# The second layer's inner products by Strassen's seven products of quarters

## The chip, the cores and the metric

The program runs on one core of one Trainium2 chip. The metric is the device time of one execution, in microseconds, as a median of several runs. TensorE multiplies a stationary 128x128 block (loaded by its own instruction, LDWEIGHTS) with a moving block and accumulates in PSUM; VectorE (DVE), ScalarE (ACT) and GpSimd (POOL) do the elementwise work; SyncE (SP) issues the transfers.

## The reference

Attention over 4 batches x 8 heads, 1152 positions of 64, with the queries averaged in pairs (576 queries), and then two feed-forward layers over the 2304 resulting tokens of width 512, each through 2048 hidden columns:

```
attn = softmax(q_pool @ k.T / sqrt(64)) @ v      # q_pool: mean of neighbouring queries
x  = attn as [2304, 512]
h  = x @ w_in      ; x = (h * cos(h))     @ w_out      # layer 1: w_in 512x2048, w_out 2048x512
h  = x @ w_in2     ; y = (h * sigmoid(h)) @ w_out2     # layer 2, same shapes
```

The weights arrive as 64-bit floats, the rest as 32-bit floats.

## The kernel before

Every operand of a product is split in two 16-bit halves, a high part and the rest (`ih`, `il` for w_in, `oh`, `ol` for w_out, `xh`, `xl` for the tokens), and a product is three matmuls: high x high, high x rest, rest x high. All scales are powers of two, taken per piece of a weight and per block of tokens from a mean or maximum that one small matmul (`bm`, L96) spreads over the partitions.

Order of work: attention with layer 1 mixed in; then the rest of layer 1; then layer 2. Tokens go in 9 blocks of 256 (the ninth gathers the remainders of the four batches). A generator `layer1` emits for every 128 hidden columns (f, 16 of them) a first product (`g1_unit`, 12 matmuls of 256 columns, L527), its evacuation by ACT (`hk`, L540), and the nonlinearity in groups of four f (L552, L553, L559, L562, L567 and POOL's `gl`, L568), and 12 units later the second product (`g2_unit1`, L586). The result of a block goes to DRAM (`ydr`) and is read back for layer 2 (`y32b`).

Layer 2's weights are prepared by the generator `weight_steps`, eight pieces of w_in2 and then eight of w_out2. A piece of 128 x 1024 wide numbers is loaded (L177, three staging buffers), decoded (ACT L206, DVE L207, L210, L215, L218), scaled (L96 to L107) and written as two halves (ACT L238, L239; POOL L240). One step of it is emitted with each remaining unit of layer 1 until w_in2 is complete (`W2.half`), and then one step with each unit of layer 2. The small matmul of a scale takes its PSUM tile from `state.psw`, which for this stage is a pool `ps_m` of its own with two buffers.

Layer 2 runs over the blocks n and over f: a first product (`g1_unit`), evacuation with Silu (L540), and for four f together the split of the result into `gh` and `gl` on DVE (`g_silu`, L574, L575). The second products (`g2_unit2`, six matmuls of 512 columns, L607, into two banks `o0`, `o1`) follow three blocks of f units later:

```
for f in range(NF):
    g1_unit(W2, cur, f)
    ...
    next(wgen2, None)
    ...
    if len(pend) > (TAIL_G - 1) * NF:
        second()
```

The split of the next block of tokens (`y_split`: maximum L112, scale, high part on ACT L890, rest on DVE L891) is emitted within the block before. The list above is a priority: a scheduler puts the instructions of each engine in a fixed order ahead of the run, and may place later work earlier where an engine would be idle by its own times. At the end stand three blocks of second products alone and the evacuation (L617) with the transfer of the output (L622).

Of the kernel before, what the change touches and what calls it, by code (L numbers as in the profile page):

```python
# [45 lines left out]
def attention_moe_moe_kernel(ctx, tc, q, k, v, w_in1, w_out1, w_in2, w_out2, out):  # L46
# [32 lines left out]
    def scale_steps(m, pool, res, top, wide=False):  # L79

        n = m.shape[1]
        if wide:
            w = small.tile([128, 1], F32, name="mw", tag="mw")
            wi, mi = w.bitcast(I32), m.bitcast(I32)
            nc.vector.tensor_scalar(
                out=wi, in0=mi, scalar1=3, scalar2=0x3F800000, op0=ALU.logical_shift_left, op1=ALU.bitwise_and
            )  # L90
            nc.vector.scalar_tensor_tensor(
                out=wi, in0=mi, scalar=1 << 30, in1=wi, op0=ALU.bitwise_and, op1=ALU.bitwise_or
            )
            m = w
        bc = pool.tile([128, 2, GW], F32, tag="h", name="bm")[:, 0, 0:4]
# [34 lines left out]
    def run_all(g):  # L130
        for _ in g:
            pass
# [11 lines left out]
    def new_w(tag, npc):  # L144
        w = Weights()
        w.npc = npc
        w.half = False
        for nm in ("si", "ui", "so", "uo"):
            setattr(w, nm, const.tile([128, npc], F32, name=nm + tag))
        w.uoT = const.tile([128, NC], F32, name="uoT" + tag)  # L150
        w.kg = const.tile([128, 1], F32, name="kg" + tag)
        w.ug = const.tile([128, 1], F32, name="ug" + tag)
        return w

    def weight_steps(w, srcs, stage, pspool, eng, nsub, bufs, ahead, wt_bufs=WT_BUFS):
# [103 lines left out]
        for e in range(r):  # L259
            pp = slice(e * (128 // r), (e + 1) * (128 // r))  # L260
            nc.vector.tensor_copy(w.uoT[pp, :], w.uo.rearrange("p (c e) -> p c e", e=r)[pp, :, e])


    class Pair:
# [211 lines left out]
    def x_scale_consts(w, s, u, first):  # L476


        c = Weights()
        n = 3 if first else TAIL_G + 1  # L480
        c.k = small.tile([128, 1], F32, tag="ck%d" % first, name="ck", bufs=n)
        c.a = small.tile([128, w.npc], F32, tag="ca%d" % first, name="ca", bufs=n)
        two_pi = 2.0 * math.pi
        nc.vector.tensor_scalar(
            out=c.k, in0=s, scalar1=w.kg, scalar2=two_pi if first else 1.0, op0=ALU.mult, op1=ALU.mult
        )
        nc.vector.tensor_scalar(
            out=c.a, in0=w.ui, scalar1=u, scalar2=0.25 / two_pi if first else 0.25, op0=ALU.mult, op1=ALU.mult
        )
        if first:  # L490
            c.y = y_scale(w, u, w.uoT, "cy1")
        return c
# [75 lines left out]
            nc.gpsimd.tensor_tensor(out=G.gl, in0=t, in1=gh, op=ALU.subtract)  # L568
        groups.clear()

    def g_silu(blk, f):
        hk = blk.hk
        gh, gl = (blk.gt[:, e, f - 3:f + 1, :] for e in range(2))
        nc.vector.tensor_scalar(out=gh, in0=hk, scalar1=blk.c.k, scalar2=None, op0=ALU.mult)  # L574
        nc.vector.scalar_tensor_tensor(out=gl, in0=hk, scalar=blk.c.k, in1=gh, op0=ALU.mult, op1=ALU.subtract)  # L575
        blk.g.append((gh, gl))

    def g2_unit1(w, blk, f):

# [20 lines left out]
    def g2_unit2(w, blk, f, pool):  # L600

        if f == 0:
            blk.y = [pool.tile([128, DM], F32, tag="o%d" % i, name="o") for i in range(2)]
        gh, gl = blk.g[f // 4]
        for i in range(2):
            for e, (gt, wt) in enumerate(((gh, w.oh), (gh, w.ol), (gl, w.oh))):
                nc.tensor.matmul(  # L607
                    blk.y[i], gt[:, f % 4, i * 128:(i + 1) * 128], wt[:, f, :],
                    start=(f == 0 and e == 0), stop=(f == NF - 1 and e == 2),
                )  # L610

    def y_evac2(W2, pool, blk, dsts):
        cy = y_scale(W2, blk.u, W2.uo, "cy0")
        for i in range(2):
            o = pool.tile([128, DM], F32, tag="x32_%d" % i, name="osb")
            np_ = W2.npc
            nc.vector.tensor_tensor(  # L617
                out=o.rearrange("p (c n) -> p c n", c=np_), in0=blk.y[i].rearrange("p (c n) -> p c n", c=np_),
                in1=cy.rearrange("p (c n) -> p c n", n=1).to_broadcast([128, np_, DM // np_]), op=ALU.mult,
            )  # L620
            for dst, p0, n in dsts[i]:
                nc.sync.dma_start(out=dst, in_=o[p0:p0 + n, :])  # L622


    if True:
        W1 = new_w("1", 8)
        alloc_w(W1, wpool, "1")
        ydr = [dram.tile([128, NC * GW], F32, name="ydr%d" % i) for i in range(2 * B + 1)]
        xrem = wpool.tile([128, B, NP * D], F32, name="xrem")

        att_stack = ExitStack()
        at = att_pools(att_stack)
# [6 lines left out]
        state.mp = None  # L639
        state.ng, state.tail = 0, False  # L640
        state.psw = ps_h
        W2 = new_w("2", 8)
        state.credit = 0.0
        bg = []
        blocks_q = []
# [146 lines left out]
        for n, (b, j) in enumerate(pairs):  # L792
# [54 lines left out]
        ps_m = ctx.enter_context(tc.tile_pool(name="ps_m", bufs=2, space=PSUM, side="right"))  # L847
# [12 lines left out]
        rb.ydst = ydr[2 * B]  # L860
        blocks_q.append(rb)

        alloc_w(W2, w2p, "2")
        state.psw = ps_m


        def y_load(n):
# [6 lines left out]
        def y_split(yb):  # L874
# [5 lines left out]
            yield from early(scale_steps(m, ps_m, (yb.s, yb.u), 14), P_CH)  # L880
            yb.blk = blk = Block()
            blk.g = []
            if yb.n:
                ys_ = state.mp.p.tile([128, 2, NC, GW], F16, tag="x%d" % (yb.n % 2), name="ys", bufs=1)
                yh, yl = ys_[:, 0], ys_[:, 1]
            else:
                ys_ = w2p.tile([128, 2, NC, GW], F16, name="ys0")
                yh, yl = ys_[:, 0], ys_[:, 1]
            yhf, ylf = yh.rearrange("p c n -> p (c n)"), yl.rearrange("p c n -> p (c n)")
# [4 lines left out]
            blk.xh = lambda c: yh[:, c, :]  # L894
            blk.xl = lambda c: yl[:, c, :]

        def y_consts(yb):
            yb.blk.c = x_scale_consts(W2, yb.s, yb.u, False)
            yb.blk.u = yb.u
            yb.blk.gt = wpool.tile([128, 2, NF, GW], F16, tag=("ih1", "il1", "oh1", "ol1")[yb.n % TAIL_G], name="gt", bufs=1)  # L900

        yb = y_load(0)
        run_all(y_split(yb))
# [24 lines left out]
        def second():  # L928
            blk, ff, nn = pend.pop(0)
            g2_unit2(W2, blk, ff, ps_o)  # L930
            if ff == NF - 1:
                y_evac2(W2, wpool, blk, out_dst(nn))

        gen = None
        for n in range(NB):
            nyb = y_load(n + 1) if n + 1 < NB else None
            gen = y_split(nyb) if nyb else None
            for f in range(NF):
                g1_unit(W2, cur, f)
                g1_evac(state.mp, W2, cur, f, False)  # L940
                if f % 4 == 3:
                    g_silu(cur, f)
                pend.append((cur, f, n))
                next(wgen2, None)
                if gen is not None and f >= 4 and next(gen, False) is False:
                    gen = None
                if len(pend) > (TAIL_G - 1) * NF:
                    second()
            if n == TAIL_G - 2:
                run_all(wgen2)  # L950
            if gen is not None:
                run_all(gen)
            if nyb:
                y_consts(nyb)
                cur = nyb.blk
        while pend:
            second()
        ctx.enter_context(moe_stack)
# [30 lines left out]
```

## Time and profile before

| | |
|---|---|
| median of 3 runs | 1409.16 us (1408.9 to 1414.57) |
| the profiled execution | 1411.62 us, of which the span of its instructions is 1409.8 us |
| mean granted clock of TensorE | 0.928 of full speed |
| busy: PE, DVE, ACT, POOL | 1162.9, 996.4, 767.5, 567.2 us |
| layer 2, from the last product of layer 1 to the end | about 1021 to 1409.8 us |

Busy time of PE is the union of matmuls that overlap each other, and a matmul's own duration is longer than the step from one to the next; steps are read from the starts in the timeline or from runs in the chain. "Idle before" is the time in which an engine waited ahead of an instruction, with what ended the wait.

### The profile page before, as it was taken

How to read it: one execution, taken by the hardware profiler on the slowest of the kernel's cores; microseconds unless marked ns; L12 is line 12 of the kernel's file. 1: busy time of each engine (PE TensorE's matmuls, PEld its weight loads, DVE VectorE, ACT ScalarE, POOL GpSimd, SP SyncE). 2: the span in 40 equal slices, each digit the busy share in tenths (PEclk: the TensorE clock that was granted, in tenths of full speed). 3: DMA queues.
4: the chain of work that ended last, by engine and by line, in shares of the span. 5: the costliest groups of instructions: out<-in, count | busy, mean ns of one | idle time of the engine just before them, and what ended most of it. 6: DMA issues, size and time to landing. Idle time of an engine off the chain costs nothing.

```text
span 1409.8 us, 24849 instructions
## 1 busy us (share of the span) xinstructions
PE 1162.9 (82%) x10020; PEld 852.0 (60%) x10020; DVE 996.4 (71%) x1848; ACT 767.5 (54%) x907; POOL 567.2 (40%) x296
## 2 busy tenths in 40 slices
PE   1465356787988778898889889979989999999998
PEld 0243233475676556666667678868878766666643
DVE  7999997778777888977999885997776323223110
ACT  3686487668777678876788775553363111111100
POOL 1577276535755466645666563552321000000000
PEclk9976568699999989998999999999999999999999
DMA  7799789987799999978899964441330000000001
GB/s 232 192 239 209 188 155 204 202 171 135 154 201 174 202 194 211 177 151 181 152 209 184 214 131 91 151 119 46 90 105 32 16 31 30 16 16 16 1 30 30
DMA packets 493074, 186.16 MB, mean 132 GB/s; under 512 B 433056, under 2 KB 467872, under 8 KB 492960
## 3 DMA queue, kind: packets, MB, share of 16 engines
q1 hardware_dynamic: 492960, 184.59, 61.7%
q8 instruction: 78, 1.28, 0.4%
q14 instruction: 36, 0.29, 0.1%
HBM read 66.58 MB, written 9.44 MB: 54 GB/s over the span
## 4 chain that ended last, share of the span: by engine, by line
PE 36%; DVE 25%; ACT 9%; issue 8%; DMA 7%; POOL 2%; SPq 2%; ACTq 0%; DVEq 0%; POOLq 0%
PE h L527 14%; PE o L607 13%; DVE sc L410 5%; PE y L586 5%; DMA hlT<-hl 3%; DVE tt L553 2%; DVE tt L552 2%; POOL hl L429 2%; PE sp L391 2%; ACT hl L424 2%; SPq L431 2%; PE pv L442 2%; DVE gh L567 1%; DVE tt L562 1%; DVE vt L311 1%
## 5 line engine op out<-in xcount | busy, mean ns | idle before, releaser
L429 POOL TENSOR_TENSOR hl<-sc,hl 128x1152 f16<-128x1152 f32 x144 | 367.8, 2563 | 189.9 <-ACT hl L424 110.8
L391 PE MATMUL sp<-kT,qT 128*128 128x512 f16 (+1 forms) x768 | 197.6, 375 | 111.2 <-DVE sc L410 86.5
L527 PEld LDWEIGHTS <-ih 128*128 128x128 f16 x2304 | 225.8, 99 | 64.6 <-issue 12.5
L410 DVE TENSOR_SCALAR_CACHE_REDUCE sc<-sp,psu 128x512 f32<-128x512 f32 (+1 forms) x288 | 229.2, 807 | 40.2 <-PE sp L391 38.8
L540 ACT ACTIVATE hk<-h,ca 128x512 f32<-128x512 f32 x144 | 97.7, 682 | 255.0 <-PE h L527 251.0
L418 ACT ACTIVATE sc<-sc,nb 128x1152 f32<-128x1152 f32 x144 | 180.3, 1252 | 95.2 <-DVE nb L415 80.6
L442 PE MATMUL pv<-vt,hlT 128*128 128x130 f16 (+1 forms) x1440 | 197.2, 239 | 39.6 <-DMA hlT<-hl 33.3
L527 PE MATMUL h<-ys,ih 128*128 128x256 f16 x1152 | 194.8, 273 | 2.9 <-ACT hk L540 2.7
L442 PEld LDWEIGHTS <-hlT 128*128 128x128 f16 (+1 forms) x1440 | 148.6, 111 | 71.0 <-DMA hlT<-hl 45.4
L527 PE MATMUL h<-xT,ih 128*128 128x256 f16 x1024 | 187.1, 276 | 4.7 <-ACT hk L540 3.9
L446 PE MATMUL pv<-vt,hlT 128*128 128x65 f16 (+1 forms) x1440 | 189.5, 209 | 0.0
L607 PE MATMUL o<-oh,gt 128*128 128x512 f16 x576 | 187.9, 379 | 1.0 <-ACT oh L238 0.6
L391 PEld LDWEIGHTS <-qT 128*128 128x128 f16 x768 | 77.9, 110 | 179.2 <-issue 137.1
L424 ACT ACTIVATE hl<-sc 128x1152 f16<-128x1152 f32 x144 | 165.5, 1157 | 18.5 <-DMA xT<-xn 8.9
L586 PE MATMUL y<-gl,oh 128*128 128x256 f16 x576 | 159.4, 277 | 3.7 <-POOL gl L568 3.7
L586 PE MATMUL y<-gh,oh 128*128 128x256 f16 x576 | 159.8, 277 | 2.5 <-ACT y L595 1.7
L586 PE MATMUL y<-gh,ol 128*128 128x256 f16 x576 | 159.7, 277 | 0.0
L527 PE MATMUL h<-ys,il 128*128 128x256 f16 x576 | 157.0, 273 | 0.0
L446 PEld LDWEIGHTS <-hlT 128*128 128x128 f16 (+1 forms) x1440 | 143.7, 108 | 16.2 <-issue 6.7
L527 PE MATMUL h<-xT,il 128*128 128x256 f16 x512 | 141.5, 276 | 0.0
L568 POOL TENSOR_TENSOR gl<-tt,gh 128x1024 f16<-128x1024 f32 x36 | 93.5, 2598 | 110.2 <-DVE gh L567 105.5
L607 PEld LDWEIGHTS <-gt 128*128 128x128 f16 x864 | 84.6, 98 | 81.3 <-issue 2.1
(281 smaller groups left out, 1884.5 us busy)
## 6 DMA issues: line engine op xcount, KB each, us to landing
wst<-in_moe_w_in_dram SPq DMA_DIRECT2D x16, 1024.0 KB, 5.7
wst<-in_moe_w_out_dram SPq DMA_DIRECT2D x16, 1024.0 KB, 6.2
stk<-in_k_dram SPq DMA_DIRECT2D x32, 288.0 KB, 4.0
stv<-in_v_dram SPq DMA_DIRECT2D x32, 288.0 KB, 4.4
stq<-in_q_dram SPq DMA_DIRECT2D x32, 256.0 KB, 3.1
ydr<-y SPq DMA_DIRECT2D x9, 512.0 KB, 3.8
y32b<-ydr SPq DMA_DIRECT2D x9, 512.0 KB, 3.3
out_dram<-osb SPq DMA_DIRECT2D x16, 256.0 KB, 2.1
```

What stands on the lines that cost most here:

```text
L391: nc.tensor.matmul(sp[:, o - a:o - a + n], P.qT[e][:, t, :], kT[:, o:o + n], start=(e == 0), stop=(e == 1))
L410: nc.vector.tensor_scalar(out=T.sc[:, a:z], in0=sp, scalar1=T.P.su, scalar2=None, op0=ALU.mult, op1=ALU.min, accum_out=mx[:, x:x + 1],)
L418: nc.scalar.activation(out=T.sc, in_=T.sc, func=AF.Exp, scale=-1.0, bias=nb)
L424: nc.scalar.activation(out=hi, in_=T.sc, func=AF.Copy)
L429: nc.gpsimd.tensor_tensor(out=T.hl[:, 1, :], in0=T.sc, in1=T.hl[:, 0, :], op=ALU.subtract)
L442: nc.tensor.matmul(G.pv[r, T.gi], T.hlT[:, 0, c, r], P.vt[i][:, c], start=(c == 0), stop=(c == KC - 1), skip_group_check=True,)
L446: nc.tensor.matmul(G.pv[r, T.gi, 0], T.hlT[:, 1, c, r], P.vt[i][:, c, 0], start=False, stop=(c == KC - 1), skip_group_check=True,)
L527: nc.tensor.matmul(hp, wt[:, c, f * 128:(f + 1) * 128], xt(c), start=(i == 0), stop=(i == 3 * NC - 1), skip_group_check=True,)
L540: nc.scalar.activation(out=o, in_=blk.hp, func=AF.Copy if first else AF.Silu, scale=blk.c.a[:, g:g + 1])
L568: nc.gpsimd.tensor_tensor(out=G.gl, in0=t, in1=gh, op=ALU.subtract)
L586: nc.tensor.matmul(blk.y[:, oc, :], wt[:, f, oc * 128:(oc + 1) * 128], gt[:, f % 4, :], start=(f == 0 and e == 0 and oc % 2 == 0), stop=(f ...
L607: nc.tensor.matmul(blk.y[i], gt[:, f % 4, i * 128:(i + 1) * 128], wt[:, f, :], start=(f == 0 and e == 0), stop=(f == NF - 1 and e == 2),)
```

## The change

The two weights' halves of w_in2 and the tokens are cut in quarters: the 512 inputs in two halves (two chunks of 128 each), the 2048 hidden columns in two halves (the even and the odd pieces of 256), the 256 tokens of a block in two halves of 128. Seven products of quarters take the place of eight, each of 128 moving columns instead of 256. The sums of quarters of the weights are formed on POOL while they are prepared (`sum_steps`, `write_pair`; seven operands in `ih`, `il`), those of the tokens on DVE in `y_split` (seven operands). `half_block` runs the seven products for half of the hidden columns, with three PSUM banks (`y`, `x`, `v`), and puts the quarters of the result together with copies on ACT and additions on DVE before Silu and the split. Two half blocks make a block.

What else moves: w_out2's halves now lie in the space of layer 1's `ih1`, `il1`; the split results `gt` in `oh1`, `ol1`, a new tile `g2w` and the tiles of layer 1's `gh`, `gl`; PSUM of `ps_m` now holds `x` and `v`, and the small matmuls of the scales take their tile from `o0` until w_in2 is complete and from layer 1's `y` (one buffer) after that. Scales of the first operands have one bit more of room (13 in place of 14), and w_in2 has one scale for two pieces. The second products follow at eight for each half block, spread over its seven steps.

The diff, cut to its core:

```diff
+        def write_pair(q, st0, st1):
+            v0, v1, f0, f1 = (x[:, :, :, z] for z in (1, 0) for x in (st0, st1))
+            for v in (v0, v1):
+                nc.scalar.activation(out=v, in_=v, func=AF.Copy, scale=w.si[:, q:q + 1])
+            sub = lambda o, x, y, op=ALU.subtract: nc.gpsimd.tensor_tensor(out=o, in0=x, in1=y, op=op)
+            hi, lo = (x.rearrange("p o c f -> p (o c) f")[:, :, q * hn:(q + 1) * hn] for x in (w.ih, w.il))
+            halves(hi[:, 0:4], lo[:, 0:4], v0)
+            yield
+            sub(f0[:, 0:2], v0[:, 0:2], v1[:, 0:2])
+            sub(v1[:, 0:2], v1[:, 0:2], v1[:, 2:4], ALU.add)
+            sub(f0[:, 2:4], v1[:, 0:2], v0[:, 0:2])
+            halves(hi[:, 4:8], lo[:, 4:8], v1)
+            yield
+            sub(f1[:, 0:2], v0[:, 2:4], f0[:, 2:4])
+            halves(hi[:, 8:12], lo[:, 8:12], f0)
+            more()
+            yield
+            halves(hi[:, 12:14], lo[:, 12:14], f1[:, 0:2])
+            more()
+            yield
...
+    def quarter_products(bank, op, xop, w, blk, u, start):
+        for i in range(4):
+            r = 4 * u + i
+            for c in range(2):
+                for wt, xt in ((w.ih, blk.xh), (w.ih, blk.xl), (w.il, blk.xh)):
+                    nc.tensor.matmul(
+                        bank[:, i, :], wt[:, op, c, r * 128:(r + 1) * 128], xt[:, xop, c, :],
+                        start=start, stop=True, skip_group_check=True,
+                    )
+                    start = False
...
+    def half_block(mp, st, w, blk, u):
...
+        y = bank("h", ps_h)
+        quarter_products(y, 0, 0, w, blk, u, True)
+        h0, h1 = (mp.p.tile([128, 4, GW], F32, tag="hk", name="hk", bufs=NB_HK) for _ in range(2))
+        copy(h0[:, :, n0], y)
+        yield
+        x = bank("x", st.psum)
+        quarter_products(x, 1, 1, w, blk, u, True)
+        add(h0[:, :, n0], x)
+        yield
+        quarter_products(y, 5, 4, w, blk, u, False)
+        copy(h0[:, :, n1], y)
+        yield
+        v = bank("w", st.psum)
+        quarter_products(v, 2, 3, w, blk, u, True)
+        yield
+        quarter_products(y, 4, 5, w, blk, u, False)
+        copy(h1[:, :, n1], y)
+        add(h1[:, :, n1], v)
+        yield
+        quarter_products(y, 3, 6, w, blk, u, False)
+        silu(blk, u, h1, y, n0)
+        silu(blk, u, h1[:, :, n1], h1[:, :, n1], slice(0, 128))
+        yield
+        quarter_products(v, 6, 2, w, blk, u, False)
+        add(h0[:, :, n1], v)
+        silu(blk, u, h0, h0, slice(0, GW))
+        g_halves(blk, u, 0, h0)
+        g_halves(blk, u, 1, h1)
+        yield
...
-                wgen2 = weight_steps(W2, (w_in2, w_out2), w2st, lambda: state.psw, nc.sync, 1, W2_BUFS, 1, 1)
+                wgen2 = sum_steps(W2, (w_in2, w_out2), w2st, lambda: state.psw, nc.sync, W2_BUFS)
...
-            nc.scalar.activation(out=yhf, in_=yb.y32, func=AF.Copy, scale=yb.s)
-            nc.vector.scalar_tensor_tensor(
-                out=ylf, in0=yb.y32, scalar=yb.s, in1=yhf, op0=ALU.mult, op1=ALU.subtract
-            )
...
+            t = state.mp.p.tile([128, 4, 2, 128], F32, tag="tt", name="yt", bufs=NB_TT)
+            for o, x, y in ((0, b12, b11), (1, b22, t[:, 0]), (2, b22, b12), (3, b21, t[:, 1])):
+                nc.vector.tensor_tensor(out=t[:, o], in0=x, in1=y, op=ALU.subtract)
+            yield
+            for o, n, x in ((0, 4, y4[:, :, 0:128]), (4, 2, b22), (6, 8, t.rearrange("p o c n -> p (o c) n"))):
+                h, lo = (z.rearrange("p o c n -> p (o c) n")[:, o:o + n] for z in (blk.xh, blk.xl))
+                nc.scalar.activation(out=h, in_=x, func=AF.Copy, scale=yb.s)
+                nc.vector.scalar_tensor_tensor(out=lo, in0=x, scalar=yb.s, in1=h, op0=ALU.mult, op1=ALU.subtract)
...
+        W2.oh, W2.ol = (wpool.tile([128, NF, DM], F16, tag=nm + "1", name=nm + "2", bufs=1) for nm in ("ih", "il"))
+        state.psw = (ps_y, "y")
...
+            for j, _ in enumerate(half_block(state.mp, st, W2, blks[n], u)):
                 next(wgen2, None)
+                if u == 0 and j > 1 and gen is not None:
+                    next(gen, None)
+                k += 8
+                while len(pend) > (TAIL_G - 1) * NF - 8 and k >= 7:
                     second()
+                    k -= 7
+            pend += [(blks[n], 8 * u + i, n) for i in range(8)]
```

Here `halves` is one ACT copy to the high half and one POOL subtraction for the rest. The decoding and scaling of a piece and the writing of w_out2's pieces are as before, one ahead of the other.

## Rows read from the trace of the kernel before

**Rows 1.** Stretches: length, each engine's busy time (instructions), clock, DMA share, GB/s.

```profile
900.00:950.00 50.00, 40.35 (x348) 34.55 (x347) 49.93 (x76) 28.11 (x31) 23.55 (x9) 0.93 0.40 116
...
1021.00:1064.00 43.00, 37.71 (x339) 32.92 (x338) 33.55 (x60) 24.86 (x30) 10.62 (x4) 1.00 0.31 93
...
1100.00:1341.00 241.00, 241.00 (x1671) 163.08 (x1670) 66.93 (x95) 37.44 (x52) 0.00 (x0) 1.00 0.05 18
```

**Rows 2.** PE's waits from 868 to 1021 us: total, times, longest.

```profile
PE bm L96 <- DVE mw L91: 7.9, 3, 6.7
PE h L527 <- ACT hk L540: 2.9, 3, 2.4
```

**Rows 3.** First products of layer 2 on the page, and their weight loads.

```profile
L527 PEld LDWEIGHTS <-ih 128*128 128x128 f16 x2304 | 225.8, 99 | 64.6 <-issue 12.5
...
L527 PE MATMUL h<-ys,ih 128*128 128x256 f16 x1152 | 194.8, 273 | 2.9 <-ACT hk L540 2.7
...
L527 PE MATMUL h<-ys,il 128*128 128x256 f16 x576 | 157.0, 273 | 0.0
```

**Rows 4.** Chain of waits in a steady block: start, length, matmuls in the run.

```profile
1216.23 2.29 PE h L527 x21
1224.05 1.31 PE h L527 x12
...
1230.69 1.32 PE o L607 x6
...
1258.05 2.29 PE h L527 x21
```

**Rows 5.** PE timeline in attention, 26 matmuls in a run: start, length.

```profile
857.71 0.19 PE L446 MATMUL pv<-vt,hlT 128*128 128x65 f16 x1
857.74 0.22 PE L442 MATMUL pv<-vt,hlT 128*128 128x130 f16 x1
...
858.76 0.19 PE L446 MATMUL pv<-vt,hlT 128*128 128x65 f16 x1
```

**Rows 6.** Groups by form from 1021 to 1064 us, the opening of layer 2.

```profile
L240 POOL TENSOR_TENSOR ol<-wst,oh 128x1024 f16<-128x1024 f32 x4 | 10.6, 2663 | 36.4 <-ACT wst L239 36.4
...
L540 ACT ACTIVATE hk<-h,ca 128x512 f32<-128x512 f32 x12 | 7.9, 683 | 5.5 <-PE h L527 3.1 <-issue 2.3
L575 DVE SCALAR_TENSOR_TENSOR gt<-hk,ck,gt 128x1024 f16<-128x1024 f32 x6 | 7.7, 1280 | 0.1
...
L112 DVE TENSOR_REDUCE ym<-y32b 128x1 f32<-128x1024 f32 x3 | 3.6, 1214 | 0.4 <-DMA y32b<-ydr 0.4
...
L207 DVE TENSOR_SCALAR_CACHE_REDUCE wt<-wt 128x1024 f32<-128x1024 f32 x2 | 2.4, 1220 | 1.3 <-ACT wt L206 1.2
```

**Rows 7.** Scales of w_out2's pieces: ns shortest/median/longest, first and last start.

```profile
L103 DVE TENSOR_SCALAR so<-uo x8: 141/145/151, 946.1 to 1062.8; 128x1 int32<-128x1 int32 x8
```

**Rows 8.** ACT timeline, the last evacuation of layer 1.

```profile
1021.27 1.57 ACT L595 ACTIVATE y<-y,cy 128x256 f32<-128x256 f32 x4 [5.24 <-PE y L586]
```

**Rows 9.** DVE timeline, one piece of w_in2 decoded.

```profile
928.73 1.22 DVE L207 TENSOR_SCALAR_CACHE_REDUCE wt<-wt 128x1024 f32<-128x1024 f32 x1
...
929.99 0.69 DVE L210 TENSOR_SCALAR wt<-wt 128x1024 int32<-128x1024 int32 x1
...
930.78 1.23 DVE L215 SCALAR_TENSOR_TENSOR wst<-wst,wt 128x1024 int32<-128x1024 int32 x1
...
932.05 1.22 DVE L218 SCALAR_TENSOR_TENSOR wst<-wst 128x1024 int32<-128x1024 int32 x1
```

**Rows 10.** Line 617, the evacuation of the output: ns shortest/median/longest.

```profile
L617 DVE TENSOR_TENSOR osb<-o,cy x18: 683/692/693, 1132.0 to 1404.6; 128x512 f32<-128x512 f32 x18
```

**Rows 11.** Line 574: ns shortest/median/longest.

```profile
L574 DVE TENSOR_SCALAR gt<-hk,ck x36: 736/753/2143, 1025.5 to 1341.6; 128x1024 f16<-128x1024 f32 x36
```

**Rows 12.** POOL timeline beside the longest of line 574, which starts at 1032.45.

```profile
1031.92 2.12 POOL L240 TENSOR_TENSOR ol<-wst,oh 128x1024 f16<-128x1024 f32 x1 [18.19 <-ACT wst L239]
```

**Rows 13.** ACT timeline, the first pieces of w_in2 written.

```profile
872.45 3.44 ACT L238 ACTIVATE ih<-wst,si 128x1024 f16<-128x1024 f32 x3
```

More of the change, by code (lines that the diff above doesn't have):

```diff
@@ L147, in new_w @@
         w.half = False
+        w.sums = sums
         for nm in ("si", "ui", "so", "uo"):
-            setattr(w, nm, const.tile([128, npc], F32, name=nm + tag))
+            n = npc // 2 if sums and nm[1] == "i" else npc
+            setattr(w, nm, const.tile([128, n], F32, name=nm + tag))
         w.uoT = const.tile([128, NC], F32, name="uoT" + tag)
@@ L261, in weight_steps, with sum_steps, shape, more @@
             nc.vector.tensor_copy(w.uoT[pp, :], w.uo.rearrange("p (c e) -> p c e", e=r)[pp, :, e])
+    def sum_steps(w, srcs, stage, pspool, eng, bufs):
+        npc = w.npc
+        hn = DFF // npc
+        srcs = [x.bitcast(I32) for x in srcs]
+        todo = [(kind, p) for kind in "io" for p in range(npc)]
+        staged = []
+        def shape(kind):
+            return (NC, DFF // npc) if kind == "i" else (NF, DM // npc)
+        def more():
+            if todo:
+                kind, p = todo.pop(0)
+                c, n = shape(kind)
+                st = stage.tile([128, c, n, 2], I32, tag="wst", name="wst", bufs=bufs)
+                eng.dma_start(
+                    out=st.rearrange("p c f z -> p c (f z)"),
+                    in_=srcs[kind == "o"][:, p * n * 2:(p + 1) * n * 2].rearrange("(c p) f -> p c f", p=128),
+                )
+                staged.append(st)
+        for _ in range(bufs):
+            more()
+        yield
+        def decode(kind, m):
+            c, n = shape(kind)
+            st = staged.pop(0)
+            t = stage.tile([128, c, n], F32, tag="wt", name="wt", bufs=1)
+            ti = t.bitcast(I32)
+            nc.scalar.activation(out=t, in_=st.bitcast(F32)[:, :, :, 1], func=AF.Abs)
+            nc.vector.tensor_scalar(
+                out=t, in0=t, scalar1=W_MIN, scalar2=None, op0=ALU.max, op1=ALU.max, accum_out=m
+            )
+            nc.vector.tensor_scalar(
+                out=ti, in0=ti, scalar1=3, scalar2=0x3FFFFFF8, op0=ALU.logical_shift_left, op1=ALU.bitwise_and
+            )
+            yield
+            v = st[:, :, :, 1]
+            nc.vector.scalar_tensor_tensor(
+                out=v, in0=v, scalar=-(1 << 30), in1=ti, op0=ALU.bitwise_and, op1=ALU.bitwise_or
+            )
+            nc.vector.scalar_tensor_tensor(
+                out=v, in0=st[:, :, :, 0], scalar=29, in1=v, op0=ALU.logical_shift_right, op1=ALU.bitwise_or
+            )
+            yield
+            return st.bitcast(F32)
+        def scales(m, s, u, top):
+            for _ in early(scale_steps(m, pspool(), (s, u), top, True), P_CH):
+                pass
+        def halves(hi, lo, t):
+            nc.scalar.activation(out=hi, in_=t, func=AF.Copy)
+            nc.gpsimd.tensor_tensor(out=lo, in0=t, in1=hi, op=ALU.subtract)
+        def first(q):
+            m = small.tile([128, 2], F32, name="wm2", tag="wm2", bufs=2)
+            return m, (yield from decode("i", m[:, 0:1]))
+        def second(q, m):
+            st = yield from decode("i", m[:, 1:2])
+            m1 = small.tile([128, 1], F32, name="wm1", tag="wm1", bufs=3)
+            nc.vector.tensor_reduce(out=m1, in_=m, axis=AX.X, op=ALU.max)
+            scales(m1, w.si[:, q:q + 1], w.ui[:, q:q + 1], 13)
+            yield
+            return st
+        def write_pair(q, st0, st1):
[16 more added lines that the diff above has]
+            halves(hi[:, 12:14], lo[:, 12:14], f1[:, 0:2])
+            more()
+            yield
+        m, st0 = yield from first(0)
+        for q in range(npc // 2):
+            st1 = yield from second(q, m)
+            nxt = None
+            if q + 1 < npc // 2:
+                nxt = yield from first(q + 1)
+            yield from write_pair(q, st0, st1)
+            if nxt:
+                m, st0 = nxt
+        nc.vector.tensor_reduce(out=w.kg, in_=w.si, axis=AX.X, op=ALU.min)
+        nc.vector.tensor_reduce(out=w.ug, in_=w.ui, axis=AX.X, op=ALU.max)
+        nc.vector.tensor_scalar(out=w.kg, in0=w.kg, scalar1=2.0**-13, scalar2=None, op0=ALU.mult)
+        nc.vector.tensor_scalar(out=w.ug, in0=w.ug, scalar1=2.0**10, scalar2=None, op0=ALU.mult)
+        w.half = True
+        def decode_o(p):
+            m = small.tile([128, 1], F32, name="wm", tag="wm", bufs=3)
+            st = yield from decode("o", m)
+            scales(m, w.so[:, p:p + 1], w.uo[:, p:p + 1], 14)
+            yield
+            return st
+        def write_o(p, st):
+            n = DM // npc
+            t, sc = st[:, :, :, 1], w.so[:, p:p + 1]
+            hi, lo = (x[:, :, p * n:(p + 1) * n] for x in (w.oh, w.ol))
+            nc.scalar.activation(out=hi, in_=t, func=AF.Copy, scale=sc)
+            nc.scalar.activation(out=t, in_=t, func=AF.Copy, scale=sc)
+            nc.gpsimd.tensor_tensor(out=lo, in0=t, in1=hi, op=ALU.subtract)
+            more()
+            yield
+        st = yield from decode_o(0)
+        for p in range(npc):
+            nst = None
+            if p + 1 < npc:
+                nst = yield from decode_o(p + 1)
+            yield from write_o(p, st)
+            st = nst
@@ L481, in x_scale_consts @@
         c.k = small.tile([128, 1], F32, tag="ck%d" % first, name="ck", bufs=n)
-        c.a = small.tile([128, w.npc], F32, tag="ca%d" % first, name="ca", bufs=n)
+        c.a = small.tile([128, w.ui.shape[1]], F32, tag="ca%d" % first, name="ca", bufs=n)
         two_pi = 2.0 * math.pi
@@ L879, in y_split @@
             yield
[L880 removed]
+            yield from early(scale_steps(m, state.psw, (yb.s, yb.u), 13), P_CH)
             yb.blk = blk = Block()
[L882 to L885, printed above, removed]
[L886 to L888 removed]
@@ new lines, in y_consts @@
+        def y_consts(yb):
+            blk = yb.blk
+            blk.c = x_scale_consts(W2, yb.s, yb.u, False)
+            blk.u = yb.u
+            z = yb.n % TAIL_G
+            if z < 3:
+                gt = g2w if z == 2 else wpool.tile([128, 2, NF, GW], F16, tag=("oh1", "ol1")[z], name="gt", bufs=1)
+                blk.gt = [[gt[:, e, 4 * j:4 * j + 4, :] for e in range(2)] for j in range(4)]
+            else:
+                blk.gt = [
+                    [state.mp.p.tile([128, 4, GW], F16, tag=nm, name=nm, bufs=NB_G) for nm in ("gh", "gl")] for _ in range(2)
+                ]
+                for j in range(2):
+                    gt = wpool.tile([128, 2, 4, GW], F16, tag="x32_%d" % j, name="gt")
+                    blk.gt.append([gt[:, e] for e in range(2)])
```

99 lines of the change are left out of this document (62 added, 37 removed).

## The prediction

> **What bounds the kernel now.** I read the stretches first, because the page's average mixes stages. From 1100 us on PE is busy without a gap (241.00 of 241.00) at full clock while DVE is busy for 28% of the time [rows 1]: this part is PE's alone. Between 900 and 950 us, where w_in2 is prepared beside the rest of layer 1, it is the other way round: DVE is busy for 49.93 of 50 us and PE for 40.35. In the opening of layer 2, 1021 to 1064 us, PE lacks 43 - 37.71 = 5.3 us and DVE works 33.55 of 43. The waits say on whom PE waited there: on the small matmul of a scale, whose operand DVE had not ready (7.9 us before 1021 us), and on ACT's evacuation of `hk` (2.9 us) [rows 2]. So a product saved is worth its whole time after 1100 us, and nothing where PE already waits for DVE. The second question is therefore what the change puts on DVE before 1100 us.
>
> **Term 1: the products.** Before there are 1152 + 576 = 1728 matmuls of 256 columns [rows 3]. In the chain 12 of them take 1.31 us, 109.2 ns each, which is 256 columns at 2.4 GHz (106.7 ns) and 2.5 ns; 188.7 us in all [rows 4]. A block takes 1258.05 - 1216.23 = 41.82 us, 16 x (1.31 + 1.30), with nothing lost. After, a half block has 7 x 4 x 2 x 3 = 168 matmuls of 128 columns, 3024 in all. The doubt is whether a matmul of 128 columns, with a weight load of its own, runs at the rate of its columns: a load shows 99 ns [rows 3], more than 128 columns need. Attention shows it: from 857.71 to 858.76 us twelve pairs of 65 and 130 columns, each matmul with its own load, take 87.5 ns a pair [rows 5]; 195 columns at 2.4 GHz are 81.25, so 3.1 ns go to each matmul, and loads overlap. For 128 columns that makes 53.3 + 3.1 = 56.4 ns; with the 2.5 ns of the long matmuls, 55.8. I take 56.4, nearest in shape: 9.47 us for a half block, 170.6 us in all, a gain of **18.1 us** (19.9 at the other end).
>
> Attention's pairs show 43.8 ns for a matmul of 97.5 columns in the mean. The Trainium skill ("TensorE: Matmul & The Clock Gate", Back-to-back issue gap) gives about 81 ns as the sustained rate of load and matmul at 128 columns in a real kernel; by that, as an estimate, 3024 would need 245 us, and the change would cost 56 us in place of gaining 18. This trace does not agree with that figure.
>
> **Term 2: the opening of layer 2.** Before, the scheduler took w_out2's pieces early: the first scale stands at 946.1 us, the last at 1062.8 [rows 7], and only 2 of 8 decodings fall after 1021 us (L207 x2, [rows 6]). After the change the small matmuls of these scales, and those of the tokens, take layer 1's PSUM tile `y`, which has one buffer and is not free before ACT has read it at 1021.27 + 1.57 = 1022.8 us [rows 8]. Without a scale no piece of w_out2 is written and no staging buffer comes free; of three buffers at most three pieces can be decoded ahead. So at least five decodings and all eight scalings come after 1022.8 us, in the stretch in which DVE also gets more for each block. What DVE has to do until w_out2 is ready, with 32 steps of the generator at 7 to a half block, that is 4.6 half blocks:
>
> - five decodings of 1.22 + 0.69 + 1.23 + 1.22 = 4.36 us [rows 9]: 21.8; eight scalings of five small instructions of 0.145 us [rows 7]: 5.8.
> - 4.6 half blocks: three additions from PSUM (a row for such an addition is missing; the multiplication of L617 has the same shape and source, 0.69 us [rows 10]) and the split of two `hk` tiles, 0.75 + 1.28 us each [rows 6, 11]: 6.13 us, together 28.2.
> - two splits of tokens: maximum 1.21, four subtractions of half of L617's size, at half its time 1.4, the rests of eight, two and eight quarters 1.28 + 0.35 + 1.28, small ones 0.9: 6.4 each, and a third maximum: 14.0.
> - POOL holds DVE up: the L574 at 1032.45 takes 2.14 instead of 0.75 us while POOL's L240 runs [rows 11, 12]. Eight L240 at 1.4 us: 11.2.
>
> The sum is 81.0 us. PE has 43.6 us of first products for 4.6 half blocks and, with two banks and two `hk` tiles, can be about a third of a half block ahead: 47. PE idles 34 us where it idled 5.3, a loss of **28.7 us**. Second products can't fill the gap, since each reads all eight pieces. Lower end: if DVE's queue cost nothing, a half block still has a chain, since both `hk` tiles are used in each: addition 0.69, Silu 1.36, split 2.03, copy 0.68 (L540's 683 ns [rows 6]), five products 6.75, and the copy between the fifth and sixth, which share a bank, 0.68: 12.2 us against 9.47, so 12.5 us idle in 4.6 half blocks, 7.2 more than before; and no more than before if the scheduler places later work into it. Upper end: POOL's stretch on every long instruction, 45 us idle, 40 more.
>
> **Term 3: w_in2's sums on POOL.** A pair of pieces now costs POOL 3.5 subtractions of full size and 4 of half size, 5.5 x 2.12 = 11.7 us [rows 12], where it cost 4.2: 30 us more over four pairs, beside 23.55 of 50 us that POOL is busy at 900 to 950 us [rows 1]. w_in2 was complete when the first scale of w_out2 came, 946.1 us [rows 7], and is needed at 1021. A pair takes some 36 us by itself, an estimate from the rows named here: ACT and POOL 22 with layer 1's `gl` in between, and the load of the next piece, its decoding and scale 14, since two of the three staging buffers are held until POOL is done. Four pairs from 872.45 us [rows 13] end near 1015: just in time. DVE is full there and is held up by POOL, but layer 1's products have 12 units of lead, and there are four scales in place of eight to hold PE's queue. I take a loss of **2 us**; ends: a gain of 5 (half of the waits of [rows 2] gone) and a loss of 18 (half of the 30 us of POOL lost on DVE, and late `gl`).
>
> **Term 4: the steady part.** The chain with four second products between (5.2 us) is 17.4 us against 9.47 + 10.4 = 19.9 us of PE, so it is covered: 0. DVE has 2 x 6.1 + 6.4 + 1.8 = 20 us in a block of 39.7. If the cover is gone because DVE's other work delays one link by over 2.5 us, it costs up to 1.5 us in each of 12 half blocks, 18 us. Additional ACT copies (0.68 each) go beside this. The last three blocks of second products are unchanged.
>
> **Sum.** -18.1 + 28.7 + 2 = +12.6 us. The profiled execution, 1411.62 us (span 1409.8), would become 1424.2; it lies 2.5 us above the median of the runs, so on the median the forecast is 1409.16 + 12.6 = **1422 us**.
>
> **The rivals.** (a) The opening is absorbed: the scheduler keeps PE in work, or DVE does more ahead of 1021 us, and PE idles little more than before. For: DVE has 43 - 33.55 = 9.5 us free in the opening [rows 1]. Against: the PSUM tile that all scales share. It decides where the added idle time is under 11 us (18.1 less the 7 that a measurement can tell): with 2 to 8 us added the time is 1395 to 1401. Faster, 23%. (b) Opening about half as bad (12 to 22 us more idle): 1405 to 1415, no change, 20%. (c) My sum, 1416.5 to 1433: 35%. (d) The chain of a half block is not covered in the steady part: forecast and 18, 1440; 10%. For: two links of DVE in it; against: 2.5 us of cover. (e) POOL delays layer 1: forecast and 16, 1438; 10%. (f) Weight loads bind matmuls of 128 columns at one load after another: 3024 x 99 = 299 us, 111 more than before, or part of it; [rows 5] exclude it all but wholly, 2%. The 81 ns of the Trainium skill's page named above (TensorE: Matmul & The Clock Gate) would be a part of this case, at 1465 us if the opening cost nothing.
>
> **Numbers.** Faster or slower by more than 0.5%, 7.0 us, is about what a measurement tells from no change. Faster 23%, same 20%, slower 57% by these cases. The range 1397 to 1443 leaves out the best half of (a), and the upper parts of (d), (e) and (f).
>
> **What would show it.** In the changed profile: twelve matmuls of 128 columns in about 0.68 us and steady blocks of 39.7 us (term 1 and 4); the first matmul of L607's successor near 1100 us instead of 1064, with PE busy about 47 of the 80 us before it and DVE near full (term 2); scales of w_out2 only after layer 1's last evacuation; w_in2's last POOL instruction near 1015 and layer 1's end near 1021 (term 3). I am wrong if w_out2 is ready by 1075, if steady blocks take over 41 us, or if layer 1 ends later than 1030.

## The result, and the profile after

The changed kernel takes 1425.68 us (1425.01 to 1426.65) against 1410.16 us of the kernel before beside it, a ratio of 1.0105 (95% interval 1.0081 to 1.0129): 15 us or 1.05% slower. Its profiled execution took 1426.28 us, span 1424.5, clock 0.921. The forecast was 12.6 us slower, 1422 us.

Stretches of the changed kernel; the columns are those of [rows 1]. Layer 1 ends at 1027.2 us, the first second product of layer 2 starts at 1101.1:

```profile
1027.20:1101.10 73.90, 52.60 (x730) 50.99 (x728) 68.73 (x125) 49.07 (x67) 15.71 (x7) 0.84 0.33 94
1101.10:1201.10 100.00, 97.64 (x1037) 68.38 (x1035) 49.89 (x80) 30.91 (x56) 2.29 (x1) 0.98 0.08 28
```

The opening is 74 us long where it was 43, DVE is busy for 68.73 us of it (93%; 78% before), and PE, which lacked 5.3 us, lacks 21.3. The granted clock of the opening is 0.84, where it was 1.00: part of the stretch is at 1.2 GHz, the lower of TensorE's two levels. Below, the chain of waits of the changed kernel in a steady stretch (to be read beside [rows 4]), where `qh`, `qx`, `qw` are the banks y, x and v and 24 matmuls are one product of quarters:

```profile
1311.75 1.34 PE qw L713 x24
1313.09 2.68 PE qh L713 x48
1315.77 3.88 PE o L805 x18
...
1332.83 2.68 PE qh L713 x48
```

24 matmuls of 128 columns take 1.34 us, 55.8 ns each, weight load included, and a half block 1332.83 - 1313.09 = 19.74 us, so a block 39.5 in place of 41.82. Two rows of the page show the counts (beside [rows 3]):

```profile
L713 PEld LDWEIGHTS <-ih 128*128 128x128 f16 x2016 | 163.3, 101 | 28.9 <-issue 19.1
...
L713 PE MATMUL qh<-ys,ih 128*128 128x128 f16 x1152 | 110.7, 225 | 11.6 <-ACT hk L739 8.1
```

In what follows "lost" is the length of a stretch less the work PE did in it at its best pace, counted from the matmuls in the groups of that stretch: 109.2 ns for 256 columns, 55.8 for 128, 215.8 for 512. It holds idle time and time at the lower clock alike. The whole, from 868 us on:

| | before | after | difference |
|---|---|---|---|
| first products of layer 2 | 188.7 | 168.7 | -20.0 |
| lost, 868 us to the end of layer 1 (1021.2; 1027.2) | 20.9 | 23.3 | +2.4 |
| lost, opening: from there to 30 us past the first second product (1064.3; 1101.1) | 7.8 | 38.4 | +30.6 |
| lost, the rest | 1.3 | 1.3 | 0 |

That is +13.0 of the 14.7 us by which the spans differ; the rest lies ahead of 868 us. Of the opening's 30.6 us, 16.0 are time in which PE is idle (21.3 as against 5.3). About 11 are inside its busy time, which is 52.6 us for 39.7 us of work at the best pace (before, 37.5 for 35.4), and about 4 fall into the 30 us behind. On whom PE waited in the opening (1021 to 1130 us; total, times, longest), beside [rows 2]:

```profile
PE qh L713 <- ACT hk L739: 8.1, 3, 4.2
PE bm L97 <- DVE mw L91: 5.3, 2, 3.1
PE qx L713 <- DVE hk L742: 3.7, 3, 1.8
PE qw L713 <- DVE hk L742: 3.0, 2, 2.3
```

L739 is the copy out of bank y and L742 the addition: the half block's own chain stands first (14.8 us in these three rows), the small matmuls of scales second. What DVE and POOL did in the opening (groups from 1027.2 to 1101.1 us), beside [rows 6, 10, 11], and w_out2's scales, beside [rows 7]:

```profile
L386 POOL TENSOR_TENSOR il<-wst,ih 128x1024 f16<-128x1024 f32 x7 | 15.7, 2244 | 59.7 <-ACT wst L385 59.7
...
L729 DVE SCALAR_TENSOR_TENSOR gt<-hk,ck,gt 128x1024 f16<-128x1024 f32 x7 | 12.5, 1792 | 0.0
...
L299 DVE TENSOR_SCALAR_CACHE_REDUCE wt<-wt 128x1024 f32<-128x1024 f32 x5 | 6.0, 1209 | 0.0
...
L742 DVE TENSOR_TENSOR hk<-hk,qw 128x512 f32<-128x512 f32 x8 | 5.4, 681 | 0.8 <-PE qw L713 0.8
```

```profile
L104 DVE TENSOR_SCALAR so<-uo x8: 141/149/155, 1030.3 to 1095.3; 128x1 int32<-128x1 int32 x8
```

Five decodings of w_out2 (L299 x5) and all eight scales fall into the opening, where two decodings did before; an addition takes 0.68 us; and L729, 1.28 us by itself, has a mean of 1.79.

### The profile page after: what moved, and what is told of

Its sections match the earlier page's. It is cut to its first block, busy times and chain, and to the rows that moved or that the text cites. A ratio compares the mean times of both kernels' runs of the same rounds, so it can differ in the third digit from the quotient of the medians.

```text
span 1424.5 us, 27673 instructions
## 1 busy us (share of the span) xinstructions
PE 1156.3 (81%) x11308; PEld 863.5 (61%) x11308; DVE 1058.9 (74%) x1938; ACT 820.1 (58%) x1023; POOL 606.9 (43%) x320
## 4 chain that ended last, share of the span: by engine, by line
PE 33%; DVE 21%; issue 12%; ACT 9%; DMA 8%; POOL 5%; SPq 1%; POOLq 0%; ACTq 0%; DVEq 0%
PE o L805 13%; PE qh L713 5%; DVE sc L545 4%; PE y L782 3%; DVE tt L688 3%; PE qw L713 3%; PE sp L526 2%; DMA hlT<-hl 2%; DMA stk<-in_k_dram 2%; PE pv L577 2%; PE h L662 2%; ACT hl L559 2%; DVE tt L687 2%; POOL hl L564 2%; DVE gh L702 2%
## 5 line engine op out<-in xcount | busy, mean ns | idle before, releaser
L526 PE MATMUL sp<-kT,qT 128*128 128x512 f16 (+1 forms) x768 | 194.6, 370 | 110.5 <-DVE sc L545 84.0
L713 PEld LDWEIGHTS <-ih 128*128 128x128 f16 x2016 | 163.3, 101 | 28.9 <-issue 19.1
L662 PEld LDWEIGHTS <-ih 128*128 128x128 f16 x1152 | 113.4, 100 | 27.6 <-issue 9.8
L703 POOL TENSOR_TENSOR gl<-tt,gh 128x1024 f16<-128x1024 f32 x36 | 89.0, 2473 | 94.9 <-DVE gh L702 94.9
L782 PEld LDWEIGHTS <-oh 128*128 128x128 f16 x1152 | 112.8, 99 | 19.0 <-issue 2.8
L713 PE MATMUL qh<-ys,ih 128*128 128x128 f16 x1152 | 110.7, 225 | 11.6 <-ACT hk L739 8.1
L805 PE MATMUL o<-ih,gt 128*128 128x512 f16 x384 | 118.6, 382 | 0.1
L713 PE MATMUL qh<-ys,il 128*128 128x128 f16 x576 | 105.8, 226 | 0.0
## 6 DMA issues: line engine op xcount, KB each, us to landing
wst<-in_moe_w_in_dram SPq DMA_DIRECT2D x16, 1024.0 KB, 6.0
wst<-in_moe_w_out_dram SPq DMA_DIRECT2D x16, 1024.0 KB, 6.5
```

Source lines behind the costliest of these rows:

```text
L526: nc.tensor.matmul(sp[:, o - a:o - a + n], P.qT[e][:, t, :], kT[:, o:o + n], start=(e == 0), stop=(e == 1))
L662: nc.tensor.matmul(hp, wt[:, c, f * 128:(f + 1) * 128], xt(c), start=(i == 0), stop=(i == 3 * NC - 1), skip_group_check=True,)
L713: nc.tensor.matmul(bank[:, i, :], wt[:, op, c, r * 128:(r + 1) * 128], xt[:, xop, c, :], start=start, stop=True, skip_group_check=True,)
L782: nc.tensor.matmul(blk.y[:, oc, :], wt[:, f, oc * 128:(oc + 1) * 128], gt[:, f % 4, :], start=(f == 0 and e == 0 and oc % 2 == 0), stop=(f ...
L805: nc.tensor.matmul(blk.y[i], gt[:, f % 4, i * 128:(i + 1) * 128], wt[:, row, :], start=(f == 0 and e == 0), stop=(f == NF - 1 and e == 2),)
```

## The experiments

The forecast's number came out, but its sum named DVE's queue as what PE waits for. Three theories were set against each other: **A**, DVE's queue, filled by w_out2's decodings that the shared PSUM tile holds back; **B**, the chain of a half block, since both `hk` tiles are used in each; **C**, w_in2's sums on POOL, which hold the staging buffers. Ratios are to the kernel before, run beside each. A half block's time is the length of the opening divided by the half blocks whose first products PE made in it (168 matmuls each), so it holds every wait of the opening. w_out2 counts as ready at the first second product. Each variant was also put in order anew by the scheduler, so a difference can hold a change of order besides the edit.

**Own bank for the scales.**

```diff
+        state.psw2 = None
...
-                wgen2 = sum_steps(W2, (w_in2, w_out2), w2st, lambda: state.psw, nc.sync, W2_BUFS)
+                wgen2 = sum_steps(W2, (w_in2, w_out2), w2st, lambda: state.psw2 or state.psw, nc.sync, W2_BUFS)
...
         state.psw = (ps_y, "y")
+        state.psw2 = (ps_o, "o1")
```

> The small matmuls of w_out2's scales take the PSUM bank o1, which is free until the first second product, in place of layer 1's y; nothing else differs. Theory A (DVE's queue in the opening, filled because the shared tile y holds all scales of w_out2 back to layer 1's end): the first scale of w_out2 comes near 990 us instead of 1030, one or two decodings and three scalings leave the opening, 6 to 10 us, so 1416 to 1420 us. Theory B (the chain of a half block sets the opening's pace): no change, 1424 to 1427. Theory C (w_in2's sums on POOL hold the staging buffers until 1010 us): the first scale is early but the other pieces come no sooner, at most 4 us gained, 1422 or more.

1.0074 (1.0047 to 1.0101), some 4 us less than the changed kernel, though the two intervals overlap. The first scale came at 1000.6 us, w_out2 was ready at 1091.4 instead of 1101.1, and a half block took as long as before (18.0 us): A in part, at the low end; the tile is not the main cause. C's gain of at most 4 us fits too, but not its condition: each of the other pieces was written 5 us or more sooner.

**Two more hk tiles in blocks 0 to 2.**

```diff
-        h0, h1 = (mp.p.tile([128, 4, GW], F32, tag="hk", name="hk", bufs=NB_HK) for _ in range(2))
+        if u == 1 and blk.n < 3:
+            h0, h1 = (wpool.tile([128, 4, GW], F32, tag="x32_%d" % i, name="hk") for i in range(2))
+        else:
+            h0, h1 = (mp.p.tile([128, 4, GW], F32, tag="hk", name="hk", bufs=NB_HK) for _ in range(2))
...
```

> In blocks 0 to 2 the second half block takes two hk tiles of its own (in space that is free there), so that a half block needn't wait for the split of the one before. Theory A: DVE is full in the opening whatever the tiles, so within 3 us of the changed kernel, 1423 to 1428. Theory B: 2.7 us in each of 4.6 half blocks come back, 10 to 12 us, 1413 to 1416.

1.0020 (1.0002 to 1.0039), 12 us less than the changed kernel, as B said and against A. Its opening, from the end of layer 1 to the first second product, as a row of the stretches:

```profile
1026.90:1105.20 78.30, 60.22 (x946) 58.38 (x944) 74.65 (x129) 53.84 (x79) 19.16 (x7) 0.93 0.31 89
```

923 first products in 78.3 us are 5.5 half blocks, 14.3 us each, where the changed kernel made 707, 4.2 half blocks, at 17.6 us. w_out2 was ready no sooner (1105.2); PE simply did more in the time, and DVE is busier still (95%). The opening lost 28.3 us as against 38.4.

**w_out2 not decoded on DVE** (with two tiles).

```diff
-            nc.vector.tensor_scalar(
-                out=ti, in0=ti, scalar1=3, scalar2=0x3FFFFFF8, op0=ALU.logical_shift_left, op1=ALU.bitwise_and
-            )
+            if kind == "i":
+                nc.vector.tensor_scalar(
+                    out=ti, in0=ti, scalar1=3, scalar2=0x3FFFFFF8, op0=ALU.logical_shift_left, op1=ALU.bitwise_and
+                )
...
```

> Three of the four DVE instructions that decode a piece of w_out2 (L302, L307, L310; 0.69 + 1.23 + 1.23 us) are left out, so w_out2 has wrong values; w_in2 is decoded in full. Theory A: five or six decodings lose 3.15 us each in the opening, 16 to 19 us, 1407 to 1410. Theory B: the chain of a half block is as long as before, under 5 us gained, 1421 or more.

1.0040 (1.0011 to 1.0068), 9 us less, between the two. The same stretch of this kernel:

```profile
1026.80:1086.20 59.40, 39.42 (x561) 38.45 (x559) 46.15 (x93) 42.43 (x57) 16.11 (x7) 0.83 0.42 116
```

w_out2 is ready 15 us sooner, so DVE's work does set that moment; but DVE is now busy for 78% only, and 539 first products are still just 3.2 half blocks at 18.5 us. The number of decodings does not set the pace of the half blocks. That does not take DVE out of the chain: followed back from 1087 us, this run's chain of work is DVE for 34.1 of 58.7 us, PE for 13.6 and ACT for 3.4. Two of its rows (start, length):

```profile
1046.78 3.07 DVE gt L731
...
1050.99 0.61 DVE hk L744
```

L731, the split that gives an `hk` tile back and for which ACT's copies waited 5.9 us in all, is drawn out from 1.27 to 3.07 us while POOL subtracts. The addition L744, for which PE waits, stands behind it and behind the first instruction of a decoding. PE works at half its rate until w_out2 is ready, so 15 us of an earlier end are worth about half: the opening lost 31.8 us as against 38.4.

**w_in2 without its sums on POOL.**

```diff
-            sub(f0[:, 0:2], v0[:, 0:2], v1[:, 0:2])
-            sub(v1[:, 0:2], v1[:, 0:2], v1[:, 2:4], ALU.add)
-            sub(f0[:, 2:4], v1[:, 0:2], v0[:, 0:2])
...
-            sub(f1[:, 0:2], v0[:, 2:4], f0[:, 2:4])
-            halves(hi[:, 8:12], lo[:, 8:12], f0)
+            halves(hi[:, 8:12], lo[:, 8:12], v0)
...
```

> The four sums of quarters of w_in2 on POOL are left out (the operands hold unsummed quarters, wrong values; all copies and rests stay): 4 x 1.06 us less POOL for each of four pairs. Theory A: the opening is as it was, layer 1 gains 0 to 3 us, 1423 to 1426. Theory C: w_in2 is complete up to 17 us sooner, the staging buffers come free as much sooner, and w_out2 with them: 1410 to 1415.

1.0074 (1.0040 to 1.0108), 4 us less, with overlapping intervals. Layer 1 ended at 1020.8 us instead of 1027.2; from its end to w_out2's readiness it took 71.3 us, and the opening lost 36.3 us as against 38.4. So the sums cost layer 1 some microseconds and the opening about 2 us. The time lies between the two ranges. POOL was done with w_in2 at 978.1 us, 34 us sooner, yet the first scale of w_out2 came only at 1024.0, since the PSUM tile `y` still held it to layer 1's end. C falls as a cause that acts alone; what an earlier w_in2 gives together with the scales' own bank was not run.

**Bank and tiles together; two steps a unit; token sums on POOL.** The second and third add to the first:

```diff
-W2_BUFS, W2_PACE, W2_N = 3, 6, 1
+W2_BUFS, W2_PACE, W2_N = 3, 6, 2
...
-                nc.vector.tensor_tensor(out=t[:, o], in0=x, in1=y, op=ALU.subtract)
+                nc.gpsimd.tensor_tensor(out=t[:, o], in0=x, in1=y, op=ALU.subtract)
```

> The own bank for w_out2's scales and the two more hk tiles together. Seen so far: the bank alone took 6 us off the changed kernel, the tiles 12, leaving out DVE's decoding 10; in the opening a half block takes 17.6 us, 18.5 with the decoding left out, 14.2 with more tiles. So theory B (the chain of a half block) is stronger than theory A (DVE's queue), and w_out2's readiness (A's scales) ends the stage. If both hold side by side: 18 us, 1407 to 1410. If DVE, 95% busy with more tiles, is what is left, the bank adds little to the tiles: 1411 to 1414.

> As with bank and tiles, and two steps of the generator with each remaining unit of layer 1 in place of one (W2_N = 2). Theory C (w_in2's preparation ends late and holds the staging buffers): w_in2 is complete 10 us or more sooner, w_out2 5 to 10 us, and the time falls by 3 to 6 us against bank and tiles. Rival: DVE, 83% busy from 900 to 1000 us, delays layer 1 by as much, 0 to 5 us worse.

> As with bank and tiles, and the four subtractions of token quarters (L1094) on POOL, which is busy for a quarter of the opening. Theory A (DVE's queue binds once the tiles are there): 1.6 us less DVE for each of two to three blocks, 3 to 4 us faster than bank and tiles. Rival: POOL's work holds DVE up for as long, and the split ends later, no gain or up to 3 us worse.

1.0026 (1.0007 to 1.0045), 1.0024 (1.0008 to 1.0041) and 1.0027 (1.0003 to 1.0051): none differs clearly from the tiles alone. With bank and tiles DVE is busy for 78.02 of 80.2 us and a half block takes 13.6 us: the time is in the range of that expectation's second reading, in which DVE's queue is what is left. That is read from DVE's load; the run with tiles and less decoding, below, bears on it. Two steps a unit did not bring what C needed: POOL ended w_in2 at 1015.9 us, and at 1015.5 with bank and tiles, so that run doesn't test C. The POOL variant took no load that mattered: DVE is busy for 76.36 of 80.5 us, POOL for 31.29.

**Matmuls that nobody reads**, to keep PE busy: `keep_busy` is called after each `quarter_products` of the half blocks 1 to 3.

```diff
+        def keep_busy():
+            old = blk.gt[:2] if u == 1 else getattr(blk, "prev", None)
+            if old is None or 2 * blk.n + u > 3:
+                return
+            junk = ps_o.tile([128, 512], F32, tag="o1", name="junk")
+            for gt in old:
+                for e in range(2):
+                    nc.tensor.matmul(
+                        junk, w.ih[:, 0, 0, 0:128], gt[e][:, 0:2, :].rearrange("p a n -> p (a n)"),
+                        start=True, stop=True, skip_group_check=True,
+                    )
...
```

> The changed kernel with matmuls whose result nobody reads (into bank o1, 512 columns, from the split results of the half block before), four after each product in the half blocks 1 to 3. In the opening the changed kernel's granted clock is 0.84 and 52.6 us of busy PE do work of 39.7 us at full clock. Theory D (the lower clock makes the chain longer): the clock in the opening rises to over 0.95, a half block takes 15 us instead of 17.6, and the time falls by 3 to 8 us, 1418 to 1423. Rival: the low clock is only a consequence, its matmuls hidden behind waits for DVE and ACT; the added matmuls then cost 0 to 6 us, 1425 to 1432.

1.0111 (1.0068 to 1.0154), as the changed kernel. The same stretch:

```profile
1028.20:1101.80 73.60, 60.15 (x755) 49.30 (x753) 66.80 (x125) 47.84 (x65) 17.29 (x8) 0.93 0.32 94
```

The clock in the opening rose from 0.84 to 0.93, and a half block took 18.8 us, no less than before. The 72 added matmuls of this stretch are 15.5 us of work at the best pace, while PE's idle time fell by only 7.9 us (from 21.3 to 13.4). So this run shows that this way of raising the clock gains nothing in all. It does not part what the clock gives from what the added matmuls cost, and the interval, of four runs, reaches into theory D's range: D is neither shown nor excluded.

**More hk tiles, and w_out2 not decoded.** The edits of two experiments above together.

> The two more hk tiles, and three of the four DVE instructions that decode w_out2 left out (wrong values). With the tiles alone a half block takes 14.2 us with DVE 95% busy; without decoding and with two tiles it took 18.5 with DVE 78% busy. Theory A after B (once the chain is loosened, DVE's queue is what remains): both ends move, w_out2 is ready near 1088 us and a half block takes 11 to 12 us; 1397 to 1403, that is the changed kernel less 23 to 28, more than tiles (12) and decoding (10) apart. Rival (the chain still sets the pace): no more than the two apart, 1404 to 1409.

0.9975 (0.9955 to 0.9996), 1405.01 us. A half block takes 12.8 us and w_out2 is ready at 1091.1, so both ends moved, but less than A after B said: the time is in the rival's range, 18 us from the changed kernel and no more than the two apart (12 + 9). PE's waits from 1025 to 1110 us (total, times, longest) still have the chain in front, with DVE busy for 84%:

```profile
PE qh L715 <- ACT hk L741: 6.9, 4, 4.1
PE qw L715 <- DVE hk L744: 3.8, 4, 1.3
```

**Block 0's second products in two or four passes** (with the tiles), so that the first pass needs only the first pieces of w_out2; the edit is shown for four.

```diff
-                    blk.y[i], gt[:, f % 4, i * 128:(i + 1) * 128], wt[:, row, :],
-                    start=(f == 0 and e == 0), stop=(f == NF - 1 and e == 2),
+                    blk.y[i][:, cols], gt[:, f % 4, i * 128:(i + 1) * 128], wt[:, row, cols],
+                    start=(f == 0 and e == 0 and part == 0), stop=(f == NF - 1 and e == 2),
...
-            pend += [(blks[n], 8 * u + i, n) for i in range(8)]
+            if n:
+                pend += [(blks[n], 8 * u + i, n, 0, 1) for i in range(8)]
+            elif u:
+                pend += [(blks[n], f, n, part, 4) for part in range(4) for f in range(NF)]
...
```

> The two more hk tiles, and block 0's second products in two passes of 256 columns each, first the left half, which needs only four of the eight pieces of w_out2. If PE's idle time in the opening is lost because nothing is ready (second products need all pieces), 10.4 us of work become ready some 35 us sooner and fill it: 1403 to 1409 against 1413 with the tiles alone. Rival: in PE's fixed order the products of the left half stand ahead of first products and hold them up: 1411 to 1416.

> As with halves, but in four passes of 128 columns, the first of which needs two pieces: 15.6 us of work for the idle time, 0.8 us more in all for the shorter matmuls. Filling theory: 1400 to 1407. Rival (holding up first products): 1411 to 1418.

Two passes: 0.9979 (0.9954 to 1.0004), 1406.75 us. Four: **0.9952 (0.9932 to 0.9972), 1403.71 us**, 0.5% faster than the kernel before and, by the two ratios, 1.5% faster than the changed one. The filling theory's ranges hold in both. With four passes second products start at 1046.3 us. PE's waits from 1025 to 1110 us, in the first fence, are then no longer the chain's: second products wait for splits (L728, L729), and the copies of a half block (L739) for next to nothing. In the 100 us from 1046.3, in the second fence, PE is idle for 6.5:

```profile
PE o L809 <- DVE gt L729: 4.2, 1, 4.2
PE o L809 <- DVE gt L728: 3.1, 1, 3.1
...
PE qh L713 <- ACT hk L739: 0.4, 1, 0.4
```

```profile
1046.30:1146.30 100.00, 93.50 (x1469) 86.89 (x1470) 83.61 (x142) 51.86 (x81) 15.69 (x6) 0.97 0.22 65
```

## Why the prediction was right, and where its working was not

**Term 1** held: 55.8 ns a matmul, where 56.4 was taken and 55.8 was the other end; 20.0 us gained against 18.1, at the best pace. The Trainium skill's 81 ns ("TensorE: Matmul & The Clock Gate", Back-to-back issue gap) is contradicted by the changed kernel itself: load and matmul of 128 columns go by in 55.8 ns in the steady part of layer 2, though a load shows 98 to 101 ns.

**Term 2** had the size (28.7 us forecast, 30.6 lost) and the moment (first second product "near 1100", measured 1101.1), and its rows came out: five decodings, eight scalings, additions of 0.68 us, POOL holding DVE up. In a row each from DVE's and POOL's timelines, L729 takes 3.15 us while POOL subtracts:

```profile
1047.49 3.15 DVE L729 SCALAR_TENSOR_TENSOR gt<-hk,ck,gt 128x1024 f16<-128x1024 f32 x1
```

```profile
1046.89 2.67 POOL L386 TENSOR_TENSOR il<-wst,ih 128x1024 f16<-128x1024 f32 x1 [3.13 <-ACT wst L385]
```

The working inside it failed in two steps, and that the number came out is in part luck.

The first is what PE does in the opening. The forecast put the loss down as idle time alone, 34 us where it was 5.3. PE was idle for 21.3 us, 16 more than before, and the rest of the 30.6 us is mostly busy time at less than the best pace, with a granted clock of 0.84 where it was 1.00. The forecast had left the clock out. Whether that time would have been idle at the full clock isn't shown.

The second is what sets the length. The sum was "what DVE has to do", 81.0 us from 1022.8 us on, with the chain of a half block as a mere lower end, 12.2 us. DVE was busy for 68.7 us, in a stretch that began at 1027.2 us, made 4.2 half blocks in place of 4.6, and left DVE idle for 5.2: the errors offset each other, so the moment came out. The runs show a length and a pace, with a cause for each. DVE's work sets when w_out2 is ready: 15 us sooner without three quarters of a decoding's instructions. What PE does until then follows the chain of a half block: 17.6 to 18.8 us with two `hk` tiles, whether DVE is busy for 93 or 78%, and 14.3 with four. The chain of 12.2 us left out the time that each link waits its turn in its engine's fixed order, on DVE above all, as the rows of the run without decoding show; how the 5 to 6 us divide among the links was not measured. ACT, which holds the copies and Silu beside w_out2's writing, was busy for 66% of the opening, and no run took load from it. The PSUM tile, which the argument leaned on, is worth about 4 us by itself, not clear of noise, and nothing measurable once the tiles are there.

**Term 3** held: 2 us forecast, 2.4 lost before the end of layer 1, and w_in2's last POOL instruction ended at 1012 us ("near 1015"). Layer 1's end moved by 6 us, which was not foreseen: besides the 2.4 us, the scheduler placed 65 first products of layer 2 (3.6 us) between 868 us and that end, where it had placed 17 of 256 columns (1.9 us), and 1.6 us more of layer 1's own products were left at 868 us. Without the sums the gain was 4 us, with overlapping intervals, so the term may have been sized a little low.

**Term 4** held: steady blocks of 39.5 us (39.7 forecast), no waits of PE after 1130 us.

Of the rivals, (a) was answered by the last experiments: it needs work for PE in the opening, and the scheduler had none to place until second products no longer needed all eight pieces. Of (b), the added idle time came out (16 us, where it said 12 to 22) but not the time, for the reason given under term 2. (d), (e) and (f) didn't come.

## What to carry to other kernels

A faster product pays only in the stage that its engine bounds; add up what the change hands to the other engines in the stage ahead of it. Where a step takes all the buffers of a stage, the next step waits for the last link of the one before, and unloading the busiest engine need not shorten it: here a half block took 18.5 us with less to decode (17.6 before) and 14.3 with the buffers doubled. Measure a step both with the buffer doubled and with the load removed before naming either. Where an engine idles for want of a complete operand, cut the work so that its first part needs only the first part of the operand: the doubled buffer brought 15 us lost down to 3, and four passes of 128 columns on top of it turned them into 7 us gained.

## What the runs showed of the hardware that was not expected

The granted clock of TensorE fell to 0.84 in the opening, where PE is idle for 21.3 of 73.9 us, and 52.6 us of busy PE did work that takes 39.7 at the best pace. Not all of the difference is the clock's: small matmuls of the scales and the ends of short runs are in the busy time too. The Trainium skill ("TensorE: Matmul & The Clock Gate", Why this matters for your kernels) advises to keep TensorE busy without gaps so as not to fall back to the lower clock; here matmuls that nobody reads brought the clock to 0.93 and no time that could be measured. That the slower matmuls stand beside waits for other engines is one possible reason; that the added matmuls cost what the clock gave is another, and no run parts them. And moving DVE's subtractions to POOL, which was busy for 14.40 of 80.2 us (18%) before the move, changed nothing that could be measured.
